# Cosine attention and a highway layer on one core: v loaded as fp32 by the hardware queues, squares and gate steps spread over engines, early products of zeros, another order

## The chip, the core and the metric

The kernel runs on one core of a Trainium2 chip. The core has five instruction queues: TensorE (PE, the matrix products; its weight loads are shown as PEld), VectorE (DVE), ScalarE (ACT), GpSimd (POOL) and SyncE (SP). SP, ACT and POOL also issue DMA transfers, which 16 DMA engines carry out. The metric is the device time of one execution in microseconds. Three timed runs of the kernel before gave 280.35, 280.48 and 280.91 us.

## The reference

Eight batches, twelve heads, 448 positions, 64 numbers per head; then a layer on 3584 rows of 768. All inputs and the result are fp32.

```python
q_n = q / (np.linalg.norm(q, axis=-1, keepdims=True) + 1e-06)
k_n = k / (np.linalg.norm(k, axis=-1, keepdims=True) + 1e-06)
scores = np.matmul(q_n, k_n.transpose(0, 1, 3, 2)) / tau        # tau = 0.1
scores = scores - np.max(scores, axis=-1, keepdims=True)
attn = np.exp(scores)
attn = attn / (np.sum(attn, axis=-1, keepdims=True) + 1e-09)
attn_out = np.matmul(attn, v)                                   # (8, 12, 448, 64)
x = attn_out.transpose(0, 2, 1, 3).reshape(8 * 448, 768)
H = np.maximum(x @ w_h, 0.0)
T = 1.0 / (1.0 + np.exp(-(x @ w_t + b_t)))
out = T * H + (1.0 - T) * x
```

## The kernel before

Work goes batch by batch (b = 0 to 7). Within a batch the twelve heads form three groups (g = 0 to 2) of four. Operands of the products are fp16, sums fp32.

For each group and for q and k: **sq** squares the tile (L359 on ACT, L362 on POOL for four of k's tiles, L364 on DVE for one half), **rd** sums the squares of a head (L370, DVE), **y** is the inverse root of these sums, by logarithm and exponent on ACT for batch 0 (L396 and L399), and by Newton steps on DVE otherwise (L381 to L388). **qn** and **kn** (L413, mostly POOL) multiply by y and make fp16. A turn brings 64-number rows onto partitions: by products with the identity (L425) and a copy from the banks (L433, DVE), or, for q from batch 3 and k from batch 5, by a transposing DMA on SP's queue (L428, tiles qT and kT).

The scores are products on TensorE (L468 and L478; L549 in batch 0), ACT takes their exponent (L471, L481, L564), TensorE multiplies with v (L499, L507, L577), where a column of ones beside v gives the sum, and DVE divides (L514, L516, L583) into x. The factor 1/tau is within the norm of q: its squares are scaled by tau before the sum.

**v** is loaded by three transfers per batch on POOL's queue (L315 to L317, into `vr`, fp16: the transfer converts). DVE (L439, **vc**) and POOL (L449, **vt**) copy it into `vp`, the layout that the product reads, with the ones and zeros around it. Both `vr` and `vp` have two buffers.

The layer has four pieces per batch, of 128 rows (the fourth half as much). x is turned by a transposing DMA on SP's queue (L628, `xT`; batch 0 by TensorE). L659 and L662 multiply with wt and wh. **za** adds the bias (L699, DVE), **th** is the hyperbolic tangent on ACT (L713), **gt** makes the gate 0.5 th + 0.5 (L715, DVE), **hm** is relu minus x (L710, DVE), **gg** multiplies (L735, DVE), **out** adds x (L737, POOL), and SP stores (L744, L747). `z` and `tt` have two buffers, `hm` three, `os` four. The last two pieces take another way (L703 to L706, L721).

All q loads stand on SP's queue, k on POOL's (batch 0: SP and ACT), w on POOL's. At the beginning TensorE runs 18 products of a tile of zeros, `wz` (L280), which DVE clears first (L264).

Nothing is scheduled at build time: each step is an operation with a number in the order in which the code makes them, `ORDER` lists these numbers in the order in which they are written into the queues, and `SLOTS` gives the buffer that each new tile takes. An engine takes its own in that order. `HOLD` puts single loads behind a named operation, and `PORT` names the kinds on DVE and POOL between which a POOL step is put behind the last DVE step ahead of it in the order.

```python
            for o in pl.ordered(ORDER, SLOTS):
                n = len(nc.cur_bb.bb.instructions)
                o.fn()
```

Of the kernel before, what the change touches and what calls it, by code (L numbers as in the profile page):

```python
# [78 lines left out]
SLOTS = {  # L79
    "qr": "01010101",  # L80
    "kr": "0120121",
    "kn": "012012021012021012102210",
    "vr": "01010101",
    "vp": "01010101",
    "sq": "012012020121021201201210120210121020120201021020",
# [94 lines left out]
def kernel(  # L180
# [110 lines left out]
    def v_src(b):  # L291
        return v[b].rearrange("h (l j) d -> l h j d", j=NJ)
# [554 lines left out]
```

## Time and profile before

| | |
|---|---|
| timed runs, median (lowest to highest) | 280.48 us (280.35 to 280.91) |
| the profiled execution: its own time / its span | 279.05 us / 277.2 us |
| mean granted TensorE clock | 0.946 |
| busy: PE, DVE, ACT, POOL | 238.2, 213.9, 204.7, 169.5 us |
| bytes read from and written to HBM | 39.12 MB, 11.01 MB |
| DMA queues: hardware (q1) / software (q0, POOL's) | 33.57 MB, 53.5% / 13.08 MB, 35.1% of 16 engines' span |

Times in the profile count from the start of the span. A group's row gives the line, the engine, the operation, the tiles out and in, their shapes and how many there were; then their busy time and the mean of one in ns; then the engine's idle time just before them and what ended it. In a row of the timeline the idle time before the instruction stands in brackets with what released it. Lines are those of the kernel before; in the kernel after the change the same code stands three lines higher or so. L12 is line 12.

### The profile page before, as it was taken

To read this page: it belongs to the slowest core of one execution; us is meant where nothing else is said; L and a number is where in the kernel's file an instruction comes from. 1 tells how busy PE (TensorE), PEld (TensorE's weight loads), DVE (VectorE), ACT (ScalarE), POOL (GpSimd) and SP (SyncE) were. 2 spreads that over 40 slices of the span, in tenths; PEclk is the share of its full clock that TensorE was granted. 3 is DMA by queue.
4 is the path that set the end of the run, shared out by engine and by line. 5 is a ranking of instruction groups with operands and counts; after the bars stand their busy time and mean duration, and the time that the engine had idled before them with its cause. 6 is when DMAs were issued, how large, how long until landed. Compare 5 with 4: busy or idle time off the path is not lost.

```text
span 277.2 us, 8206 instructions
## 1 busy us (share of the span) xinstructions
PE 238.2 (86%) x3447; PEld 146.5 (53%) x3447; DVE 213.9 (77%) x367; ACT 204.7 (74%) x253; POOL 169.5 (61%) x161
## 2 busy tenths in 40 slices
PE   8256799699989899498896999997999989999990
PEld 3135676365755565255554466564645755575640
DVE  3889669779999988639997678789776766446894
ACT  3396898799998989658788599996889568870230
POOL 2495829939837899138879645789348941330550
PEclk9856599999999999979999899999999999999998
DMA  7999599998599769996889979999879467238565
GB/s 229 290 176 254 161 246 204 216 275 104 60 162 263 115 177 223 135 197 120 125 228 166 201 136 175 194 272 196 113 177 163 82 147 162 66 75 194 139 154 144
DMA packets 77398, 47.93 MB, mean 173 GB/s; under 512 B 53040, under 2 KB 74160, under 8 KB 77360
## 3 DMA queue, kind: packets, MB, share of 16 engines
q1 hardware_dynamic: 54128, 33.57, 53.5%
q0 software_dynamic: 22800, 13.08, 35.1%
q10 hardware_dynamic: 432, 0.75, 0.8%
q8 instruction: 27, 0.44, 0.7%
q14 instruction: 11, 0.09, 0.1%
HBM read 39.12 MB, written 11.01 MB: 181 GB/s over the span
## 4 chain that ended last, share of the span: by engine, by line
PE 43%; DMA 21%; DVE 15%; POOL 10%; issue 6%; ACT 2%; DVEq 0%; POOLq 0%; ACTq 0%
PE banks L662 22%; DMA xT<-x 9%; PE banks L468 6%; PE banks L499 6%; DMA kr<-in_k_dram 6%; PE banks L659 4%; DMA qT<-qn 4%; POOL qn L413 3%; POOL kn L413 3%; DVE tt L715 2%; DVE hm L735 2%; DMA qr<-in_q_dram 2%; ACT E L471 2%; DVE x L516 2%; PE banks L478 1%
## 5 line engine op out<-in xcount | busy, mean ns | idle before, releaser
L471 ACT ACTIVATE E<-banks 128x896 f16<-128x896 f32 x126 | 109.7, 917 | 22.0 <-PE banks L468 20.0
L662 PEld LDWEIGHTS <-xT 128*128 128x128 f16 x576 | 51.9, 99 | 49.9 <-issue 14.1
L737 POOL TENSOR_TENSOR os<-x,hm 128x768 f32<-128x768 f16 (+1 forms) x30 | 44.7, 1493 | 42.9 <-DVE hm L735 20.2
L662 PE MATMUL banks<-wt,xT 128*128 128x384 f16 x288 | 55.3, 333 | 7.0 <-DMA xT<-x 6.9
L662 PE MATMUL banks<-wh,xT 128*128 128x384 f16 x288 | 55.6, 332 | 0.9 <-DVE hm L710 0.9
L370 DVE TENSOR_REDUCE n<-sq 128x14 f32<-128x896 f32 (+1 forms) x50 | 51.1, 1037 | 6.3 <-ACT sq L359 6.3
L413 POOL TENSOR_TENSOR qn<-qr,y 128x896 f16<-128x896 f32 (+1 forms) x24 | 41.0, 1710 | 23.2 <-issue 10.8
L413 POOL TENSOR_TENSOR kn<-kr,y 128x384 f16<-128x384 f16 (+1 forms) x42 | 40.0, 964 | 21.5 <-DVE y L388 7.8
L468 PE MATMUL banks<-qT,kT 64*64 64x448 f16 x504 | 40.0, 365 | 2.8 <-DVE x L516 1.7
L713 ACT ACTIVATE tt<-z 128x768 f16<-128x768 f32 (+1 forms) x32 | 24.2, 764 | 19.8 <-DVE z L699 19.2
L499 PE MATMUL banks<-vp,E 128*128 128x65 f16 x756 | 37.7, 194 | 0.0
L499 PEld LDWEIGHTS <-E 128*128 128x128 f16 x756 | 34.0, 97 | 6.5 <-issue 3.6
L710 DVE SCALAR_TENSOR_TENSOR hm<-banks,x 128x768 f16<-128x768 f32 (+1 forms) x30 | 25.7, 858 | 13.1 <-PE banks L662 10.2
L499 PE MATMUL banks<-vp,Et 128*128 128x65 f16 x252 | 34.3, 192 | 0.0
L699 DVE TENSOR_TENSOR z<-banks,bias 128x768 f32<-128x768 f32 x24 | 22.9, 952 | 9.6 <-PE banks L662 9.4
L359 ACT ACTIVATE sq<-qr 128x896 f32<-128x896 f32 (+1 forms) x24 | 22.1, 935 | 5.3 <-DMA qr<-in_q_dram 3.7
L499 PEld LDWEIGHTS <-Et 128*128 128x128 f16 x252 | 24.9, 99 | 0.0
L715 DVE TENSOR_SCALAR tt<-tt 128x768 f16<-128x768 f16 (+1 forms) x32 | 21.8, 683 | 2.7 <-ACT tt L713 2.7
L516 DVE TENSOR_TENSOR x<-banks,rd 128x896 f16<-128x896 f32 x21 | 22.9, 1089 | 0.5
L481 ACT ACTIVATE Et<-banks 128x896 f16<-128x896 f32 x21 | 19.0, 917 | 4.5 <-PE banks L478 4.4
L468 PEld LDWEIGHTS <-kT 64*64 64x64 f16 x504 | 12.6, 105 | 17.7 <-issue 15.2
L359 ACT ACTIVATE sq<-kr 128x896 f32<-128x896 f16 x17 | 16.1, 951 | 5.1 <-DMA kr<-in_k_dram 4.7
(74 smaller groups left out, 301.4 us busy)
## 6 DMA issues: line engine op xcount, KB each, us to landing
out_dram<-os SPq DMA_DIRECT2D x47, 192.0 KB, 3.3
qr<-in_q_dram SPq DMA_DIRECT2D x6, 1344.0 KB, 7.4
kr<-in_k_dram POOLq DMA_DIRECT2D x7, 672.0 KB, 12.9
vr<-in_v_dram POOLq DMA_DIRECT2D x8, 384.0 KB, 7.7
qr<-in_q_dram SPq DMA_DIRECT2D x6, 448.0 KB, 6.8
vr<-in_v_dram POOLq DMA_DIRECT2D x8, 288.0 KB, 9.4
out_dram<-os SPq DMA_DIRECT2D x15, 96.0 KB, 2.6
wt<-in_moe_w_t_dram POOLq DMA_DIRECT2D x1, 1152.0 KB, 13.8
```

The lines of the kernel that those rows point to most:

```text
L359: nc.scalar.activation(dst, src, AF.Square, scale=sc)
L370: nc.vector.reduce_sum(R("n2", b)[:, c : c + 7 * n], a, axis=AX.X)
L413: ENG[eng].tensor_mul(o[:, :, t0:t1, :], a, y.unsqueeze(3).to_broadcast([128, hi - lo, t1 - t0, D]))
L468: nc.tensor.matmul(R("B", ("S", n, c))[64 * x : 64 * x + 64, t, 0:S], lhsT=keys(i, s, t, 2 * c + x), rhs=queries(t, s), start=True, stop=True)
L471: op("ACT", f"exp {n} {c}", lambda c=c, n=n: nc.scalar.activation(R("E", n)[:, 14 * c : 14 * c + 14, :].rearrange("l (t j) x -> l t (j x)" ...
L499: nc.tensor.matmul(U[:, 2 * c + t, :], lhsT=(E if m < NC else Et)[:, at : at + 2, :].rearrange("l j x -> l (j x)"), rhs=vp[:, 3 * t + m if ...
L516: op("DVE", f"ev14 {i}", lambda: nc.vector.tensor_mul(R("x", b)[:, :, 128 * g : 128 * g + 128].rearrange("l j (s d) -> l s j d", s=2), U_( ...
L662: nc.tensor.matmul(R("B", at)[:, mh, 0:MH], lhsT=xT[:, cc, :], rhs=w_[:, cc, MH * mh : MH * mh + MH], start=(cc == 0), stop=(cc == CC - 1))
L710: step("hm", n, lambda n=n, P=P: nc.vector.scalar_tensor_tensor(out=cut(R("hm", g), n), in0=P(n), scalar=0.0, in1=xs(n), op0=ALU.max, op1= ...
L713: op("ACT", f"th{nb} {g}", lambda: nc.scalar.activation(R("tt", g)[:, 0:W], R("z", g)[:, 0:W], AF.Tanh, scale=0.5), r=[("z", g), ("t0",)], ...
L715: op("DVE", f"gt{nb} {g}", lambda: nc.vector.tensor_scalar(out=R("tt", g)[:, 0:W], in0=R("tt", g)[:, 0:W], scalar1=0.5, scalar2=0.5, op0=A ...
L737: op("POOL", f"out{nb} {g}", lambda: nc.gpsimd.tensor_add(view(R("os", g)), xs(None), view(R("hm", g))), r=[("gg", g), xk], w=[("os", g)], ...
```

## The change

1. `vr` becomes fp32, and its three loads per batch leave POOL's queue: 22 of 24 go to SP's, two to ACT's. The copies into `vp` convert to fp16, five of DVE's vc now run on POOL, and one of POOL's vt on DVE.
2. A table, `MOVED`, sets another engine for 46 operations. Of 48 tiles of squares (beside the split ones of group 0 of batch 0) 12 are on POOL and 7 on DVE, where POOL had four and DVE none; ten of 24 wide gate steps and four of eight narrow ones go from DVE to POOL; three loads of q go from SP's queue to ACT's.
3. The squares are no longer scaled by tau; the exponent of the scores multiplies by 1/tau instead. On DVE a square is now a plain product of two operands.
4. After the 18 products of zeros stand 23 more, and two times six later among the first products.
5. `ORDER`, `SLOTS` and `HOLD` are new throughout, and gg is no longer among `PORT`. The operands of the final addition are swapped.

```diff
--- before
+++ after
-1 4 24 25 2 6 26 0 242 21 17 27 14 19 29 3 16 18 12 28 9 22 13 5 8 11 40 15 20 42 7 10 43 36 38 41 37 39 52 53 44 68
...
+3 24 25 242 26 0 27 2 29 28 4 30 9 31 7 6 32 13 15 240 11 5 16 12 21 19 22 40 42 18 14 8 41 20 38 10 1498 1499 1500
+1501 1502 1503 1504 1505 1506 1507 1508 1509 1510 1511 1512 1513 1514 1515 1516 1517 1518 1519 1520 36 39 43 37 44 52
...
 SLOTS = {
...
-HOLD = {239: 44, 240: 57, 241: 252, 429: 121, 610: 56, 788: 57, 966: 53, 1141: 537, 1316: 161}
-PORT = ("nt", "gt", "gg", "vc", "qn", "kn", "vt", "out", "cx", "ou")
+HOLD = {240: 0, 429: 107, 610: 53, 966: 795, 1141: 89, 1316: 843}
+MOVED = {'sq1 q 0 0 1': 'ACT', 'sq1 k 0 0 1': 'DVE', 'sq2 q 0 1 0': 'POOL', 'gt6 0': 'POOL', 'gt6 1': 'POOL', 'gt6 2': 'POOL', 'gt3 3': 'POOL', 'ldq 1 0': 'ACT', 'ldq 1 2': 'ACT', 'sq2 q 1 1 0': 'POOL', 'sq2 q 1 2 0': 'POOL', 'vc6 1 0 1': 'POOL', 'gt6 4': 'POOL', 'gt3 7': 'POOL', 'sq2 q 2 0 0': 'DVE', 'sq2 k 2 2 0': 'POOL', 'gt6 9': 'POOL', 'sq2 q 3 1 0': 'DVE', 'sq2 k 3 1 0': 'POOL', 'sq2 k 3 2 0': 'POOL', 'vc6 3 0 1': 'POOL', 'ldq 4 0': 'ACT', 'sq2 k 4 1 0': 'DVE', 'sq2 k 4 2 0': 'POOL', 'gt6 16': 'POOL', 'gt6 18': 'POOL', 'ldv4 5': 'ACT', 'sq2 k 5 0 0': 'POOL', 'sq2 k 5 2 0': 'POOL', 'vc6 5 0 1': 'POOL', 'gt6 20': 'POOL', 'gt6 21': 'POOL', 'gt3 23': 'POOL', 'sq2 q 6 1 0': 'DVE', 'sq2 q 6 2 0': 'POOL', 'sq2 k 6 2 0': 'DVE', 'vc6 6 0 0': 'POOL', 'vt 6 0': 'DVE', 'ldv4 7': 'ACT', 'sq2 k 7 0 0': 'DVE', 'sq2 q 7 1 0': 'DVE', 'sq2 k 7 1 0': 'POOL', 'sq2 k 7 2 0': 'POOL', 'vc6 7 0 1': 'POOL', 'gt6 30': 'POOL', 'gt3 31': 'POOL'}
+PORT = ("nt", "gt", "vc", "qn", "kn", "vt", "out", "cx", "ou")
...
     def op(self, eng, name, fn, w=(), r=(), u=(), mode=None):
-        o = Op(eng, name, fn, w, r, u, mode)
+        o = Op(MOVED.get(name, eng), name, fn, w, r, u, mode)
         o.seq = len(self.ops)
...
-    WARM, FILL, NLATE = 18, (), 2
+    WARM, FILL, NLATE = 18, (23, 6, 6), 2
...
-        qr=(2, [128, 6, 448], FP32), kr=(3, [128, 6, 448], FP16), kn=(3, [128, NJ, 2, D], FP16), vr=(2, [128, NH, 256], FP16),
+        qr=(2, [128, 6, 448], FP32), kr=(3, [128, 6, 448], FP16), kn=(3, [128, NJ, 2, D], FP16), vr=(2, [128, NH, 256], FP32),
...
+    on = []
...
-                ENG[eng].dma_start(d[:, :, :], a)
+                on[-1].dma_start(d[:, :, :], a)
             else:
-                ENG[eng].dma_start(d[:, gs[0] :: 3, :], a[:, :, gs[0] :: 3, :])
+                on[-1].dma_start(d[:, gs[0] :: 3, :], a[:, :, gs[0] :: 3, :])
         op(eng, f"ld{nm} {b} {gs[0]}", fn, w=[(nm + "r", b, g) for g in gs])
...
-            (4, lambda: nc.gpsimd.dma_start(vr()[0:64].rearrange("l h (c d) -> l h c d", c=4), v_src(b)[:, :, 0:4, :])),
-            (3, lambda: nc.gpsimd.dma_start(vr()[64:128, :, 0:192].rearrange("l h (c d) -> l h c d", c=3), v_src(b)[:, :, 4:7, :])),
-            (1, lambda: nc.gpsimd.dma_start(vr()[64:128, 1::2, 192:256], v_src(b)[:, 1::2, 3, :]))):
-            op("POOL", f"ldv{n} {b}", fn, w=[("vr", b, n)])
+            (4, lambda: on[-1].dma_start(vr()[0:64].rearrange("l h (c d) -> l h c d", c=4), v_src(b)[:, :, 0:4, :])),
+            (3, lambda: on[-1].dma_start(vr()[64:128, :, 0:192].rearrange("l h (c d) -> l h c d", c=3), v_src(b)[:, :, 4:7, :])),
+            (1, lambda: on[-1].dma_start(vr()[64:128, 1::2, 192:256], v_src(b)[:, 1::2, 3, :]))):
+            op("SP", f"ldv{n} {b}", fn, w=[("vr", b, n)])
...
-    SQV = ()
-    SQP = tuple(("k", b, 1) for b in range(2, 6))
...
         i = (nm, b, g)
-        sc = tau if nm == "q" else 1.0
-        engs = SPLIT.get(i, (("DVE" if i in SQV else "POOL" if i in SQP else "ACT"),))
+        engs = SPLIT.get(i, ("ACT",))
         n = 3 - len(engs)
         for t, eng in enumerate(engs):
             ts = slice(t, t + n)
 
-            def fn(eng=eng, ts=ts):
+            def fn(ts=ts):
                 src = source(nm, b, g)[:, ts]
                 dst = R("sq", i).rearrange("l (t x) -> l t x", t=2)[:, ts]
-                if eng == "ACT":
-                    nc.scalar.activation(dst, src, AF.Square, scale=sc)
-                elif eng == "POOL":
-                    assert sc == 1.0
-                    nc.gpsimd.tensor_mul(dst, src, src)
+                if on[-1] is nc.scalar:
+                    nc.scalar.activation(dst, src, AF.Square)
                 else:
-                    nc.vector.scalar_tensor_tensor(out=dst, in0=src, scalar=sc * sc, in1=src, op0=ALU.mult, op1=ALU.mult)
+                    on[-1].tensor_mul(dst, src, src)
             op(eng, f"sq{n} {nm} {b} {g} {t}", fn, r=[token(nm, b, g), ("t6",)], w=[("sq", i, t)])
...
-                nc.vector.tensor_copy(
+                on[-1].tensor_copy(
                     R("vp", b)[:, p0:p1, 3 * t : 3 * t + 3, 0:D],
                     R("vr", b)[:, 6 * t + p0 : 6 * t + p1, 0:192].rearrange("l p (c d) -> l p c d", c=NC))
...
-                    R("E", n)[:, 14 * c : 14 * c + 14, :].rearrange("l (t j) x -> l t (j x)", t=2), R("B", ("S", n, c))[:, :, 0:S], AF.Exp),
+                    R("E", n)[:, 14 * c : 14 * c + 14, :].rearrange("l (t j) x -> l t (j x)", t=2), R("B", ("S", n, c))[:, :, 0:S], AF.Exp, scale=1.0 / tau),
...
-                op("DVE", f"gt{nb} {g}", lambda: nc.vector.tensor_scalar(
+                op("DVE", f"gt{nb} {g}", lambda: on[-1].tensor_scalar(
                     out=R("tt", g)[:, 0:W], in0=R("tt", g)[:, 0:W], scalar1=0.5, scalar2=0.5, op0=ALU.mult, op1=ALU.add),
...
-        op("POOL", f"out{nb} {g}", lambda: nc.gpsimd.tensor_add(view(R("os", g)), xs(None), view(R("hm", g))),
+        op("POOL", f"out{nb} {g}", lambda: on[-1].tensor_add(view(R("os", g)), view(R("hm", g)), xs(None)),
            r=[("gg", g), xk], w=[("os", g)], u=[("hm", g)])
...
+    for i, n in enumerate(FILL):
+        for j in range(n):
+            op("PE", f"wf {i} {j}", constant(("F", i)), r=[("wz",)], w=[("B", ("F", i))], mode="F")
...
             for o in pl.ordered(ORDER, SLOTS):
                 n = len(nc.cur_bb.bb.instructions)
+                on.append(ENG[o.eng])
                 o.fn()
```

More of the change, by code (lines that the diff above doesn't have):

```diff
@@ L93 @@
-    "Et": "012012021021021021021",
+    "qn": "012012012012012012012012",
+    "qT": "01230123012301203123012",
+    "kT": "01230123012301230213021",
+    "E": "012012121020102000210210210210120120210210121021012012012",
+    "Et": "012012012012010210210",
     "rd": "010101010101010101010101010101010",
     "x": "012012012",
-    "xT": "01234021342013420143241302143201",
-    "z": "01011010011010101010101000101010",
-    "tt": "01010100100110101010010010110101",
-    "hm": "01202012201201201201201202102012",
@@ L283 @@
         op("PE", f"wm {i}", constant(("W",)), r=[("wz",)], w=[("B", ("W",)), ("wm",)], mode="F")
-    for i, n in enumerate(FILL):
-        for j in range(n):
-            op("PE", f"wf {i} {j}", constant(("F", i)), r=[("wz",)], w=[("B", ("F", i))], mode="F")
     def q_src(t, b):
@@ L481, in scores @@
         op("ACT", f"expt {i}", lambda: nc.scalar.activation(
-            R("Et", i).rearrange("l (t j) x -> l t (j x)", t=2), R("B", ("St", i))[:, :, 0:S], AF.Exp),
+            R("Et", i).rearrange("l (t j) x -> l t (j x)", t=2), R("B", ("St", i))[:, :, 0:S], AF.Exp, scale=1.0 / tau),
            r=[("B", ("St", i))], w=[("Et", i)])
@@ L564, in fe @@
                 nc.scalar.activation(R("E", e).rearrange("l j x -> l (j x)")[:, o : o + 2 * m].rearrange("l (t x) -> l t x", t=2),
-                                     R("B", A)[:, :, 0:m], AF.Exp)
+                                     R("B", A)[:, :, 0:m], AF.Exp, scale=1.0 / tau)
             op("ACT", f"ex{wide(ss[0]) // 64} {n}", fe, r=[("B", A)], w=[("E", e, s) for s in ss] + [("E", e, 0)])
```

28 lines of the change are left out of this document (14 added, 14 removed), and 108 rows, old and new, of the table ORDER.

## Prediction

> **What bounds the kernel now.** I read the page first, then busy time in stretches of 4 us, then the chain of waits and the timeline at the places where TensorE stands still, and last the groups that the change moves.
>
> ```profile
> span 277.2 us, 8206 instructions
> PE 238.2 (86%) x3447; PEld 146.5 (53%) x3447; DVE 213.9 (77%) x367; ACT 204.7 (74%) x253; POOL 169.5 (61%) x161
> PE 43%; DMA 21%; DVE 15%; POOL 10%; issue 6%; ACT 2%; DVEq 0%; POOLq 0%; ACTq 0%
> ```
>
> TensorE is the fullest engine, yet the chain that ended last lies on it for only 43% and on DMA for 21%. So I look for the 39 us (277.2 less 238.2) in which it is idle. Columns of the next view: stretch, its length, busy time (instructions) of PE, PEld, DVE, ACT, POOL, then granted clock, DMA share, GB/s.
>
> ```profile
> 8.00:12.00 4.00, 0.00 (x0) 0.00 (x0) 3.36 (x7) 2.19 (x4) 1.10 (x1) 0.96 1.16 280
> 12.00:16.00 4.00, 2.49 (x39) 1.97 (x42) 2.97 (x5) 1.62 (x3) 4.00 (x7) 0.50 1.02 239
> 16.00:20.00 4.00, 2.00 (x48) 1.49 (x39) 3.55 (x4) 3.97 (x9) 3.53 (x4) 0.50 1.37 166
> 20.00:24.00 4.00, 2.89 (x44) 2.20 (x45) 3.77 (x7) 4.00 (x7) 3.80 (x4) 0.50 1.17 216
> 48.00:52.00 4.00, 2.86 (x40) 1.61 (x39) 1.94 (x5) 1.68 (x3) 3.94 (x4) 1.00 1.47 196
> 112.00:116.00 4.00, 1.82 (x44) 1.09 (x43) 3.76 (x10) 3.57 (x5) 0.00 (x0) 1.00 1.40 163
> 116.00:120.00 4.00, 2.14 (x11) 1.13 (x12) 0.00 (x0) 0.00 (x0) 0.00 (x0) 0.69 1.37 200
> 148.00:152.00 4.00, 1.92 (x49) 1.32 (x43) 3.04 (x4) 3.92 (x5) 3.64 (x4) 0.95 1.28 141
> 188.00:192.00 4.00, 2.05 (x31) 1.11 (x33) 4.00 (x4) 1.68 (x3) 3.80 (x4) 1.00 1.24 206
> 240.00:244.00 4.00, 4.00 (x51) 2.07 (x49) 2.41 (x5) 3.69 (x5) 0.00 (x0) 1.00 0.00 0
> ```
>
> Three kinds of loss: a start (8 to 24 us) with TensorE half idle and its clock at 0.50; a hole at 48 to 52; holes at 112, 148 and 188 where the DMA share is above 1.2. From 240 on TensorE is full at full clock, so what is gained earlier reaches the end.
>
> **The start.** The second head group's norms, not POOL, set the pace, and ACT's queue delays them:
>
> ```profile
> 12.19 0.93 PE L425 MATMUL banks<-ident,qn 128*128 128x128 f16 x7 [5.12 <-POOL qn L413]
> 10.12 0.23 ACT L399 ACTIVATE y<-tu 128x28 f32<-128x28 f32 x1
> 12.25 0.57 DVE L413 TENSOR_TENSOR kn<-E,y 128x192 f16<-128x192 f32 x1
> 14.41 0.95 ACT L359 ACTIVATE sq<-kr 128x896 f32<-128x896 f16 x1 [2.38 <-DMA kr<-in_k_dram]
> 16.44 0.23 ACT L399 ACTIVATE y<-tu 128x28 f32<-128x28 f32 x1
> 16.75 1.70 POOL L413 TENSOR_TENSOR qn<-qr,y 128x896 f16<-128x896 f32 x1 [0.47 <-ACT y L399]
> ```
>
> ACT waits 2.38 us for k of batch 1 while the squares and the logarithm of group 1 stand behind that wait; POOL's scaling of group 1 starts only when y is there (16.67). ACT's rows, before:
>
> ```order
> L399 ACTIVATE y_78<-tu_81 128x28
> L359 ACTIVATE sq_75<-qr_61 128x896
> L359 ACTIVATE sq_73<-E_95 128x896
> L359 ACTIVATE sq_74<-kr_63 128x896
> L359 ACTIVATE sq_75<-E_96 128x896
> L396 ACTIVATE tu_82<-n_76,eps 128x28
> L399 ACTIVATE y_78<-tu_82 128x28
> ```
>
> and of the change, from the same y on:
>
> ```order
> L396 ACTIVATE y_78<-tu_81 128x28
> L359 ACTIVATE sq_73<-E_95 128x896
> L305 DMA qr_62<-in_q_dram 128x2x448
> L359 ACTIVATE sq_74<-E_96 128x896
> L393 ACTIVATE tu_82<-n_76,eps 128x28
> L396 ACTIVATE y_78<-tu_82 128x28
> L305 DMA qr_62<-in_q_dram 128x2x448
> L359 ACTIVATE sq_75<-qr_61 128x896
> L359 ACTIVATE sq_73<-kr_63 128x896
> ```
>
> The square of q group 1 went to POOL, and the one of batch 1's k stands behind group 1's y. Without that wait y of group 1 is set by Vector's work after y of group 0. That one came at 10.35; now a square of half a tile, about 0.6, moves from Vector's queue behind the first sum to ACT, so 9.8. Then come two scalings like the one at 12.25 (1.2 together), two sums of squares at 1.07 (row below), and logarithm and exponent at about 0.55: 13.7, or 3.0 us earlier. Against it stand the early products:
>
> ```profile
> 1.26 5.81 PE L280 MATMUL banks<-wz 128*128 128x512 f16 x18 [1.26 <-DVE wz L264]
> 2.62 1.15 DVE L264 MEMSET vp<- 128x36 f16 x4 [0.17 <-issue]
> 4.97 1.61 PEld L280 LDWEIGHTS <-wz 128*128 128x128 f16 x8 [0.17 <-issue]
> ```
>
> The zero tile is now cleared behind eight memsets of vp (two such groups, 2.3 us), so products start near 3.6 instead of 1.26. Of the 53, 40 stand ahead of the first transposes. Before, ten of 18 took the first 3.71 us (4.97 less 1.26) and eight the next 1.61, 0.20 each. So ten slow ones to 7.3 and 30 fast ones to 13.3: the first transposes start 1.1 us later than 12.19, and 13 more products (2.6 us) stand between the next ones. In return those run at full clock: the 7.4 us of work in the three rows at 0.50 shrink by up to half, 3.7. I count these two as even.
>
> The Trainium skill, "TensorE: Matmul & The Clock Gate", Part 1, says the activity window is free-running at some 3.4 us. By it the full clock may come one to two windows after 3.6, an estimate of 7.0 to 10.4, and the 40 products would end at 13.4 to 15.2; the trace's 3.71 lies within, and no run here shows the spread.
>
> **The hole at 48.** Pieces of the chain (start, us, what), and the instruction that waited:
>
> ```profile
> 34.07 16.36 DMA kr<-in_k_dram
> 50.51 1.79 ACT L359 ACTIVATE sq<-kr 128x896 f32<-128x896 f16 x2 [2.32 <-DMA kr<-in_k_dram]
> 108.16 9.66 DMA xT<-x
> 143.12 8.46 DMA xT<-x
> 191.65 6.86 DMA qT<-qn
> ```
>
> The k load of batch 2 is issued at 34.07 and lands 16.36 us later, behind wh and among v. POOL's rows before:
>
> ```order
> L413 TENSOR_TENSOR kn_66<-kr_63,y_79 128x4x128
> L317 DMA vr_70<-in_v_dram 64x6x64
> L321 DMA wh<-in_moe_w_h_dram 128x6x768
> L300 DMA kr_64<-in_k_dram 128x6x448
> L316 DMA vr_70<-in_v_dram 64x12x192
> L315 DMA vr_70<-in_v_dram 64x12x256
> ```
>
> and of the change:
>
> ```order
> L410 TENSOR_TENSOR qn_85<-qr_61,y_78 128x896
> L324 DMA wh<-in_moe_w_h_dram 128x6x768
> L361 TENSOR_TENSOR sq_75<-qr_62 128x896
> L361 TENSOR_TENSOR sq_74<-qr_62 128x896
> L303 DMA kr_64<-in_k_dram 128x6x448
> L303 DMA kr_65<-in_k_dram 128x6x448
> L410 TENSOR_TENSOR kn_66<-kr_63,y_79 128x3x128
> ```
>
> The load (kr_64) now stands ahead of batch 1's scaling, behind two squares (3.4 us), and no v is in that queue: about 27 (13.7, and 13.3 us of scalings, squares, casts and two weight issues on POOL ahead of it, an estimate from their rows). Even at 16.36 us it lands at 43, so ACT's 2.32 us of waiting goes. ACT also loses two squares of this stretch (1.8). First term: 3.0 at the start, of which ACT's full row (16 to 24) passes on perhaps half, 1.5; plus 2.3; plus little of the squares, since DVE is nearly as full: **-4**, bounds -7 and 0.
>
> **The holes at 112, 148, 188.** There the transposes on SP's queue are slow: 9.66, 8.46 and 6.86 us, where the median is 3.6. What ran beside the first:
>
> ```profile
> 108.01 0.89 POOL L300 DMA_DIRECT2D kr<-in_k_dram  x1
> 108.89 0.77 POOL L316 DMA_DIRECT2D vr<-in_v_dram  x1
> xT<-x SPq DMA_TRANSPOSE x28, 3.6
> vr<-in_v_dram POOLq DMA_DIRECT2D x8, 384.0 KB, 7.7
> ```
>
> k and v go out in one burst. The change separates v from k, but puts it ahead of transposes. SP before, from batch 4's q on:
>
> ```order
> L300 DMA qr_61<-in_q_dram 128x6x448
> L428 DMA_TRANSPOSE qT_86<-qn_84 128x7x128
> L628 DMA_TRANSPOSE xT_106<-x_104 128x3x128
> L744 DMA out_dram<-os_119 64x384 x2
> L300 DMA qr_62<-in_q_dram 128x6x448
> L428 DMA_TRANSPOSE qT_87<-qn_83 128x7x128
> ```
>
> and now at the same transposes:
>
> ```order
> L743 DMA out_dram<-os_118 64x768 x2
> L319 DMA vr_69<-in_v_dram 64x12x192
> L425 DMA_TRANSPOSE qT_86<-qn_83 128x7x128
> L320 DMA vr_69<-in_v_dram 64x6x64
> L319 DMA vr_70<-in_v_dram 64x12x192
> L740 DMA out_dram<-os_120 64x384 x2
> L303 DMA qr_62<-in_q_dram 128x6x448
> ```
>
> Five times a large piece of v stands right ahead of a transpose. The bytes read are the same; those written into the tile double. TensorE's idle time in the rows at 112, 116, 148 and 188 is 8.0 us. I take a third of it back: **-3**, bounds -8 (all) and +10 (five transposes each late by 7.7 less 3.6, half of it on the path).
>
> **Work moved between engines.**
>
> ```profile
> L370 DVE TENSOR_REDUCE n<-sq 128x14 f32<-128x896 f32 x46 | 48.9, 1074 | 3.1 <-ACT sq L359 3.1
> L737 POOL TENSOR_TENSOR os<-x,hm 128x768 f32<-128x768 f16 x23 | 38.3, 1671 | 35.1 <-DMA out_dram<-os 15.8 <-DVE hm L735 13.2 <-DVE tt L715 6.0
> L715 DVE TENSOR_SCALAR tt<-tt 128x768 f16<-128x768 f16 x24 | 18.1, 759 | 2.1 <-ACT tt L713 2.1
> L439 DVE COPY vp<-vr 128x1152 f16<-128x1152 f16 x14 | 9.2, 657 | 0.0
> L449 POOL COPY vp<-vr 64x384 f16<-64x384 f16 x16 | 8.3, 520 | 7.9 <-DVE hm L735 4.6 <-issue 1.3 <-DMA vr<-in_v_dram 0.7
> L362 POOL TENSOR_TENSOR sq<-kr 128x896 f32<-128x896 f16 x4 | 6.7, 1676 | 3.9 <-DVE n L370 3.8
> L316 POOL DMA_DIRECT2D vr<-in_v_dram x8 | 6.2, 771 | 0.0
> L315 POOL DMA_DIRECT2D vr<-in_v_dram x8 | 6.2, 772 | 0.0
> L439 DVE COPY vp<-vr x18: 338/453/1899, 24.0 to 233.0; 128x1152 f16<-128x1152 f16 x14, 128x576 f16<-128x576 f16 x4
> ```
>
> POOL loses 24 issues of v, a third kind beside the two rows being like them, some 18 us, and gains eight squares (13.4), ten wide and four narrow gate steps and five casts. No row has its one-input price at 768: twice the 0.52 for 384 gives 1.04 below, the two-input 1.67 above; I take 1.04, the nearest kind. That is 12.5, and the casts (three times 0.52) 7.8: POOL goes from 169.5 to 185, to 198 at the top. ACT loses 15 squares (14) and issues five loads. DVE loses ten gate steps at 0.76, four narrow ones and five copies at 0.66, gains seven squares at about 1.07, and its nine wide casts cost 0.66 if they run like the copy, 1.38 if like the sum of squares (1.074 over 896, for 1152): between -5 and +3. None becomes the fullest. What may show is the gate: a step on POOL can wait behind a scaling, so I add **+1.5**, bounds 0 and +9. The scale of 1/tau in the exponent and the swapped operands of the final sum add no instruction.
>
> The Trainium skill, "SBUF — State Buffer", Who interferes with whom, says POOL and two-port Vector copies or casts lock each other out for a whole instruction. The 1,899 ns copy beside a median of 453 agrees. More POOL work is then a loss at DVE too; by it the +1.5 would be nearer its upper bound.
>
> **Sum.** -4 -3 +1.5 = -5.5 on the profiled execution: 279.05 (span 277.2 and 1.85 around it) becomes 273.55. The three timed runs have their median 1.43 above that execution, so 280.48 becomes **275.0**.
>
> **Rivals.**
> - All three losses go (start -6, holes -6.5, gate +0.5): 268.5. For it: TensorE has 39 us to give. Against: every byte still has to move. 0.15.
> - The early products are in the way: the first transposes wait until 15 and the start gains nothing; -3 +1.5 gives 279. For it: 40 products in a row. 0.12.
> - The gain is handed back, other transposes being late instead: 280.5. 0.06.
> - Slower: v ahead of transposes in SP's ring. Start -4, holes 0, five late transposes cost 4.1 each, and with a third on the path +7, gate +1.5: 285. It decides against the change once more than 0.5 us of each 4.1 reaches TensorE. 0.12.
> - Slower: gates on POOL at 1.67, each behind one scaling (1.7): 14 times 2.6 us late, of which a quarter, +9, reaches TensorE through two-deep rings: 282.5. 0.12.
> - The forecast, 272 to 278: 0.43.
>
> Within 0.2% is what a measurement here cannot tell from no change. Faster 0.43 + 0.15 + 0.12 = 0.70, same 0.06, slower 0.24. The range cuts the outer half of the best case and most of the worst: 268.5 to 283.5; the forecast's own is 272 to 278.
>
> **What would show it.** Right: group 1's y near 13.7; no hole at 48; a clock near 1.0 from 12 to 24; fewer transposes over 8 us; POOL near 185. Wrong: first transposes after 15; ACT idle behind late exponents; transposes waiting directly behind v; POOL's gate step above 1.5 us or DVE waiting for it.

## The result

| | before | predicted | after |
|---|---|---|---|
| time, median of five runs | 280.48 us (280.19 to 280.91) | 275.0 us (268.5 to 283.5; the forecast's own 272 to 278) | 277.04 us (276.24 to 278.47) |
| ratio to before | | 0.980 | 0.988, 95% interval 0.985 to 0.991 |
| the profiled execution | 279.05 us | 273.55 us | 278.47 us, the longest of its five |

The change makes the kernel faster, by 3.4 us where 5.5 were forecast. On a second chip its ratio was 0.992 (0.987 to 0.996, the last experiment), so the gain is 0.8 to 1.2%. One execution of a later kernel took 332.78 us at a granted clock of 0.656, and the ratios leave out such executions and all that lie over 1.5% above the shortest of their kernel on that chip.

The two profiled executions are only 0.58 us apart: the one of before is shorter than all its five timed runs, the one of the change is the longest of its five. Their traces show what moved, but not where the 3.4 us of the medians come from. The page of the profile after:

```profile
span 276.7 us, 8304 instructions
PE 241.6 (87%) x3482; PEld 148.9 (54%) x3482; DVE 223.9 (81%) x356; ACT 194.5 (70%) x238; POOL 182.3 (66%) x163
PE 42%; DVE 28%; DMA 10%; POOL 9%; issue 6%; SPq 3%; ACT 1%; DVEq 0%; POOLq 0%; ACTq 0%
```

The third row is the chain that ended last. DMA's share of it fell from 21% to 10%, Vector's rose from 15% to 28% (12% and 32% in a second profile of the change, the last experiment). The stretches of 4 us that the prediction showed of before, in the kernel after (same columns, core's busy time of PE, PEld, DVE, ACT, POOL, then clock, DMA share, GB/s):

```profile
16.00:20.00 4.00, 3.45 (x50) 2.23 (x48) 3.06 (x5) 3.03 (x6) 2.30 (x4) 1.00 1.12 238
20.00:24.00 4.00, 2.09 (x81) 1.59 (x80) 4.00 (x7) 4.00 (x6) 2.27 (x3) 1.00 1.13 242
24.00:28.00 4.00, 1.98 (x39) 1.82 (x39) 4.00 (x6) 1.54 (x2) 3.87 (x4) 0.61 1.15 230
28.00:32.00 4.00, 3.54 (x78) 3.08 (x76) 4.00 (x11) 2.56 (x4) 2.57 (x3) 0.50 1.16 212
48.00:52.00 4.00, 3.89 (x73) 2.80 (x72) 4.00 (x7) 3.39 (x5) 4.00 (x4) 1.00 1.16 236
112.00:116.00 4.00, 4.00 (x39) 2.04 (x37) 4.00 (x8) 3.55 (x5) 2.95 (x4) 1.00 1.24 176
148.00:152.00 4.00, 4.00 (x34) 1.79 (x33) 4.00 (x8) 2.52 (x4) 3.85 (x4) 1.00 1.04 213
188.00:192.00 4.00, 4.00 (x46) 2.24 (x43) 3.92 (x5) 3.06 (x4) 3.71 (x5) 1.00 0.79 163
```

The holes at 48, 112, 148 and 188 are gone. The start is not: the clock is full until 24, but TensorE is half idle from 20 to 28, and the clock is at 0.61 from 24 and at 0.50 from 28, which it had before from 12 to 24. The stretch became shorter as well as later: the clocks of the seven rows from 12 to 40 us add up to a loss worth 20 us at half clock before and 14 us after. And the rest has changed sides more than once. First the kernel before, then the kernel after, in three longer stretches:

```profile
56.00:112.00 56.00, 53.39 (x848) 33.19 (x850) 51.84 (x86) 52.49 (x65) 43.34 (x40) 1.00 0.92 171
112.00:160.00 48.00, 38.94 (x508) 22.34 (x507) 35.96 (x56) 33.72 (x42) 31.29 (x26) 0.93 1.00 168
200.00:240.00 40.00, 39.00 (x545) 23.04 (x542) 27.06 (x46) 30.39 (x38) 23.29 (x22) 1.00 0.72 138
```

```profile
56.00:112.00 56.00, 49.19 (x781) 31.64 (x780) 53.16 (x77) 46.47 (x57) 43.91 (x38) 1.00 1.03 219
112.00:160.00 48.00, 42.60 (x603) 24.78 (x604) 44.66 (x67) 38.19 (x46) 39.62 (x33) 1.00 1.13 191
200.00:240.00 40.00, 37.19 (x510) 21.89 (x507) 20.05 (x32) 28.33 (x37) 22.48 (x21) 0.96 0.81 140
```

TensorE lost 4.2 us from 56 to 112, gained 3.7 from 112 to 160 and lost 1.8 from 200 to 240. The holes at the transposes were filled, and many small waits came ahead of them. By the view of waits TensorE stood 10.1 us behind DMA before and 7.5 after, but 9.8 behind Vector before and 12.5 after (sums of the rows by releaser). Of the latter, 1.3 and 3.9 us are the first product's wait for the tile of zeros; without it the sums are 8.5 and 8.6. What grew is Vector's part from 56 to 112, from 1.8 to 4.0 us.

The longest DMA pieces in the chain, which were 16.36, 9.66 and 8.46 us, are now these:

```profile
152.05 6.78 DMA xT<-x
187.07 7.05 DMA vr<-in_v_dram
204.88 8.08 DMA out_dram<-os
216.42 5.55 DMA kT<-kn
```

The third of them is a store, and it hands part of the gain back. POOL's final sum waits until the store lands and its tile is free, the scaling of k stands behind that sum on POOL, and k's transpose, the fourth piece, behind the scaling. Of the 3429 products that both kernels share, 2896 had started by 220 us in the change and 2832 before; by 230 us it was 2967 and 2969, and up to the end the two profiled executions stay level. The same store is long in other kernels with the new order too (7.84 us in the second profile of the change).

### The profile page after: what moved, and what is told of

Its sections match the earlier page's. It is cut to its first block, busy times and chain, and to the rows that moved or that the text cites. A ratio compares the mean times of both kernels' runs of the same rounds, so it can differ in the third digit from the quotient of the medians.

```text
span 276.7 us, 8304 instructions
## 1 busy us (share of the span) xinstructions
PE 241.6 (87%) x3482; PEld 148.9 (54%) x3482; DVE 223.9 (81%) x356; ACT 194.5 (70%) x238; POOL 182.3 (66%) x163
## 4 chain that ended last, share of the span: by engine, by line
PE 42%; DVE 28%; DMA 10%; POOL 9%; issue 6%; SPq 3%; ACT 1%; DVEq 0%; POOLq 0%; ACTq 0%
PE banks L659 16%; DVE n L367 6%; PE banks L496 5%; PE banks L465 5%; PE banks L656 4%; PE banks L285 4%; POOL kn L410 3%; POOL qn L410 3%; DMA out_dram<-os 3%; DMA vr<-in_v_dram 3%; DVE vp L436 3%; DMA xT<-x 2%; DVE hm L731 2%; DVE hm L707 2%; DMA kT<-kn 2%
## 5 line engine op out<-in xcount | busy, mean ns | idle before, releaser
L659 PEld LDWEIGHTS <-xT 128*128 128x128 f16 x576 | 51.1, 97 | 45.8 <-issue 12.1
L733 POOL TENSOR_TENSOR os<-hm,x 128x768 f32<-128x768 f16 (+1 forms) x30 | 44.6, 1493 | 30.4 <-DVE hm L731 16.9
L659 PE MATMUL banks<-wt,xT 128*128 128x384 f16 x288 | 54.0, 327 | 3.5 <-DMA xT<-x 3.2
L410 POOL TENSOR_TENSOR kn<-kr,y 128x384 f16<-128x384 f16 (+1 forms) x42 | 40.6, 983 | 17.5 <-DVE y L385 6.9
L496 PE MATMUL banks<-vp,E 128*128 128x65 f16 x756 | 38.4, 194 | 0.0
L465 PEld LDWEIGHTS <-kT 64*64 64x64 f16 x504 | 13.4, 104 | 26.5 <-issue 21.0
L561 ACT ACTIVATE E<-banks 128x1024 f16<-128x1024 f32 (+2 forms) x21 | 18.5, 917 | 6.7 <-PE banks L574 3.7
L731 DVE TENSOR_TENSOR hm<-tt,hm 128x768 f16<-128x768 f16 (+1 forms) x30 | 20.7, 693 | 1.4 <-POOL tt L712 1.2
L285 PE MATMUL banks<-wz 128*128 128x512 f16 x53 | 13.8, 422 | 3.9 <-DVE eps L269 3.9
## 6 DMA issues: line engine op xcount, KB each, us to landing
kr<-in_k_dram POOLq DMA_DIRECT2D x7, 672.0 KB, 10.3
vr<-in_v_dram SPq DMA_DIRECT2D x8, 576.0 KB, 10.3
```

The lines of the kernel that those rows point to most:

```text
L285: return lambda: nc.tensor.matmul(R("B", at)[:, 0, :], lhsT=wz[:, 0:128], rhs=wz[:, 128:640], start=True, stop=True)
L410: on[-1].tensor_mul(o[:, :, t0:t1, :], a, y.unsqueeze(3).to_broadcast([128, hi - lo, t1 - t0, D]))
L465: nc.tensor.matmul(R("B", ("S", n, c))[64 * x : 64 * x + 64, t, 0:S], lhsT=keys(i, s, t, 2 * c + x), rhs=queries(t, s), start=True, stop=True)
L496: nc.tensor.matmul(U[:, 2 * c + t, :], lhsT=(E if m < NC else Et)[:, at : at + 2, :].rearrange("l j x -> l (j x)"), rhs=vp[:, 3 * t + m if ...
L659: nc.tensor.matmul(R("B", at)[:, mh, 0:MH], lhsT=xT[:, cc, :], rhs=w_[:, cc, MH * mh : MH * mh + MH], start=(cc == 0), stop=(cc == CC - 1))
L731: op("DVE", f"gg{nb} {g}", lambda: nc.vector.tensor_mul(R("hm", g)[:, 0:W], R("tt", g)[:, 0:W], R("hm", g)[:, 0:W]), r=[("gt", g), ("hm", ...
```

## The experiments

On the experiments' chips the executions of one kernel lie up to 2% from their median (274.15 to 286.29 us around 280.16 in one). So the ratios to the kernel before on the same chip decide, and where few executions stand behind one the single times are given.

### The extra products: left out, and started earlier

```diff
-    WARM, FILL, NLATE = 18, (23, 6, 6), 2
+    WARM, FILL, NLATE = 18, (), 2
```

(and the numbers 1498 to 1532 out of `ORDER`, with their banks in `SLOTS`.)

> The changed kernel without its 35 extra products of zeros; the 18 early ones stay. Theory (the extra products hold TensorE until 14.6 us, later than y of group 1 allows): the first transposes start near 12.5 us in place of 14.45, the clock is 0.50 from 12 to about 20, and the time falls by 1 to 2 us, to 275.0 to 276.0. Rival (the two effects cancel, as the prediction counted them): 276.6 to 277.5. Second rival (the extra products pay through the clock): 278 to 280.

The second kernel clears the zero tile, operation 4, first on Vector:

```diff
-3 24 25 242 26 0 27 2 29 28 4 30 9 31 7 6 32 13 15 240 11 5 16 12 21 19 22 40 42 18 14 8 41 20 38 10 1498 1499 1500
+4 3 24 25 242 26 0 27 2 29 28 30 9 31 7 6 32 13 15 240 11 5 16 12 21 19 22 40 42 18 14 8 41 20 38 10 1498 1499 1500
```

> The changed kernel with one memset moved: the zero tile of the products is cleared ahead of the vp memsets on Vector, as before the change. The products then start near 1.3 in place of 3.9 us and end near 12 to 12.5. Theory (the late end of the products costs): first transposes near 12.5 to 13.5, time 275.5 to 276.3. Rival (group 2's late q load, not group 1, sets the first 28 us): y of group 2 stays at 19.9 and the time at 276.7 to 277.5.

Measured: 277.32 us, ratio 0.985 (0.978 to 0.992), and 279.11 us, ratio 0.988 (0.979 to 0.998). Neither differs from the whole change by what can be told, so the rivals hold by the ratio. By the single time 279.11 us is above both ranges of the second experiment, and its rival's condition was not met either: y of the third group came at 18.6, not 19.9. TensorE's timeline in the change, without the products, and with the zeros first:

```profile
3.91 10.70 PE L285 MATMUL banks<-wz 128*128 128x512 f16 x40 [3.91 <-DVE eps L269]
14.45 0.55 PE L422 MATMUL banks<-ident,qn 128*128 128x128 f16 x7
26.42 0.93 PE L422 MATMUL banks<-ident,qn 128*128 128x128 f16 x7 [2.02 <-POOL qn L410]
```

```profile
11.46 0.55 PE L419 MATMUL banks<-ident,qn 128*128 128x128 f16 x7 [1.03 <-POOL ident masks.py:199]
26.54 0.93 PE L419 MATMUL banks<-ident,qn 128*128 128x128 f16 x7 [3.05 <-POOL qn L407]
```

```profile
11.78 0.55 PE L422 MATMUL banks<-ident,qn 128*128 128x128 f16 x7
26.24 0.93 PE L422 MATMUL banks<-ident,qn 128*128 128x128 f16 x7 [2.90 <-POOL qn L410]
```

The first transposes move by 3 us, from 14.45 to 11.46 or 11.78, and those of the third q group start at 26.2 to 26.5 in all three. Before the change that group was turned at 23.86. What makes it late stands on POOL, in the kernel after (two rows), without the products, and with the zeros first:

```profile
24.03 0.54 POOL L446 CAST vp<-vr 64x384 f16<-64x384 f32 x1 [1.76 <-DMA vr<-in_v_dram]
24.65 1.71 POOL L410 TENSOR_TENSOR qn<-qr,y 128x896 f16<-128x896 f32 x1
```

```profile
24.12 0.57 POOL L443 CAST vp<-vr 64x384 f16<-64x384 f32 x1 [3.01 <-DMA vr<-in_v_dram]
```

```profile
23.81 0.50 POOL L446 CAST vp<-vr 64x384 f16<-64x384 f32 x1 [2.83 <-DMA vr<-in_v_dram]
```

In the change the third group's y is there at 19.9 (before 20.2), and POOL waits 1.76 us for v ahead of the scaling of q, which began at 22.09 before. Where y comes sooner, POOL only waits longer for v. v's three transfers of this batch, which landed by 20.67 before, land at about 23.9 in all three. With v back in POOL's queue (below) the third group is turned at 25.16, so v is a cause of its lateness. It does not set the whole time: that kernel is 2.5 us ahead of the change at 40 us and level with it at 44.

### Vector relieved: squares to ScalarE, gates back to Vector, all engines as before

Three kernels change entries of `MOVED`. In the first the seven squares of DVE go back to ACT (`...` leaves entries out):

```diff
-MOVED = {... 'sq2 q 2 0 0': 'DVE', ... 'sq2 q 3 1 0': 'DVE', ... 'sq2 k 7 0 0': 'DVE', 'sq2 q 7 1 0': 'DVE', ...}
+MOVED = {...}
```

> The changed kernel with its seven squares of Vector back on ScalarE (order as it is). Theory (Vector at 53 of 56 us from 56 to 112 has become the full engine): DVE's busy time falls by 9 to 10 us to about 214, ACT's grows by 6.5 to 201, and the time falls by 2 to 4 us to 273 to 275. Rival (ScalarE, at 93% in the same stretch, takes the place, or the waits for scores grow): 277 to 279.

In the second the gate steps and wide casts of POOL go back to DVE:

```diff
-MOVED = {... 'gt6 0': 'POOL', 'gt6 1': 'POOL', 'gt6 2': 'POOL', 'gt3 3': 'POOL', ... 'vc6 7 0 1': 'POOL', ...}
+MOVED = {...}
```

> The changed kernel with its 14 gate steps and five casts of v that went to POOL back on Vector. POOL falls from 182 to about 166. Theory (Vector is the full engine from 56 to 160): DVE's busy time grows by 8 to 13 us and the time by 3 to 5 us, to 280 to 282. Rival (POOL's two-input work beside Vector costs Vector as much as it takes off it): Vector's other steps shorten, DVE grows by under 5 us, and the time is 276 to 278.

In the third every moved operation goes back to its engine before:

```diff
-MOVED = {'sq1 q 0 0 1': 'ACT', ... 'gt3 31': 'POOL'}
+MOVED = {'sq2 k 2 1 0': 'POOL', 'sq2 k 3 1 0': 'POOL', 'sq2 k 4 1 0': 'POOL', 'sq2 k 5 1 0': 'POOL'}
```

> The changed kernel with the engines of before: squares on ScalarE but for four on POOL, gate steps, wide casts of v on Vector, q loads on SP; v stays in fp32 on SP's queue, and the order and the extra products stay. Theory (the moves cost, +1.5 in the prediction, nearer its bound of +9 by Vector's grown time): ratio to before 0.975 to 0.985. Rival (ScalarE was the engine that had to be relieved): ScalarE at 205 and the ratio 0.992 to 1.002.

Measured: squares to ACT 279.19 us, ratio 0.989 (0.980 to 0.998); gates to DVE 279.83 us beside 281.69 of before, 276.67 to 281.95 and no interval; engines as before 277.91 us, ratio 0.991 (0.988 to 0.994). None is told from the change; by the ratio the first is where its rival put it, and the third lies between its two ranges, next to the rival's. The theory that Vector had become the bound is not borne out. Squares to ACT took Vector from 223.9 to 217.0 us busy, and TensorE did no more from 56 to 112 than in the change (48.45 us of 56 beside 49.19, in an execution of 282.99 us, the longest of its four), but Vector itself went only from 53.16 to 51.13 us in that stretch. More telling is the kernel before: Vector was as full there, 51.84 us, with TensorE at 53.39. Gates to DVE brought Vector to 229.2 us, 5.3 more, between what theory and rival had, and POOL down to 166.1 as expected; its two shortest executions took 276.67 and 278.76 us. With all engines as before TensorE had 49.04 us from 56 to 112, the busy times being

```profile
PE 241.4 (87%) x3482; PEld 148.9 (54%) x3482; DVE 215.6 (78%) x367; ACT 204.8 (74%) x253; POOL 152.1 (55%) x137
```

So moving 46 operations took 10.3 us off ScalarE, put 30.2 on POOL and 8.3 on Vector, and left the time where it was. Vector got more although about as much was taken off it as was added: by the rows with the engines as before, ten wide and four narrow gate steps and five casts, some 11 us, for squares and a cast of some 10. In the change, and with the engines as before:

```profile
L712 DVE TENSOR_SCALAR tt<-tt 128x768 f16<-128x768 f16 x14 | 9.5, 677 | 1.8 <-ACT tt L710 1.8
L378 DVE TENSOR_SCALAR y<-n 128x84 int32<-128x84 int32 x6 | 3.6, 601 | 0.0
```

```profile
L712 DVE TENSOR_SCALAR tt<-tt 128x768 f16<-128x768 f16 x24 | 11.8, 492 | 2.2 <-ACT tt L710 2.1
L378 DVE TENSOR_SCALAR y<-n 128x84 int32<-128x84 int32 x6 | 1.2, 195 | 0.0
```

The means hide two kinds of step. Of the six small steps of 84 columns in the change four take 192 to 198 ns, and two take 1144 and 1683. These two start while a step of POOL runs and end 0.06 us after it, as the later one shows:

```profile
157.14 1.68 POOL L361 TENSOR_TENSOR sq<-kr 128x896 f32<-128x896 f16 x1 [0.35 <-POOL qn L410]
157.20 1.68 DVE L378 TENSOR_SCALAR y<-n 128x84 int32<-128x84 int32 x1
```

With the engines as before none of the six meets a step of POOL, and all take 187 to 204 ns. The wide gate step, too, takes 342 to 360 ns where it meets none and up to 1887 in the change where it meets one. So what counts is what a step meets, which the order sets, not how much POOL has to do in all: the kernel before, with 169.5 us on POOL, has 439 for the small step, and the same changed kernel profiled again has 703, and 861 for the gate step. The 2.3 us that the row of gate steps gave back for ten steps fewer lie within that spread (9.5 and 12.1 us for the same fourteen).

### The path of v: POOL's queue in the new order, SP's in the old

```diff
-        vr=(2, [128, NH, 256], FP32),
+        vr=(2, [128, NH, 256], FP16),
...
+MOVED = {... 'ldv4 0': 'POOL', 'ldv3 0': 'POOL', 'ldv1 0': 'POOL', ... 'ldv1 7': 'POOL'}
```

> The changed kernel with v as before: loaded as fp16 through POOL's queue (24 issues), its copies on chip fp16 to fp16; order, engines and extra products of the change. Theory (taking v off POOL's queue is what made the holes smaller, the prediction's -3): POOL at about 198 busy, DVE about 216, the holes return and the ratio to before is 0.997 to 1.005. Rival (the path of v is neutral, the gain came from the order): 0.984 to 0.992, as with the whole change.

and the kernel before with this part alone:

```diff
-        vr=(2, [128, NH, 256], FP16),
+        vr=(2, [128, NH, 256], FP32),
...
-            (4, lambda: nc.gpsimd.dma_start(vr()[0:64].rearrange("l h (c d) -> l h c d", c=4), v_src(b)[:, :, 0:4, :])),
+            (4, lambda: nc.sync.dma_start(vr()[0:64].rearrange("l h (c d) -> l h c d", c=4), v_src(b)[:, :, 0:4, :])),
...
-            op("POOL", f"ldv{n} {b}", fn, w=[("vr", b, n)])
+            op("SP", f"ldv{n} {b}", fn, w=[("vr", b, n)])
```

> The kernel before with one part of the change: v in fp32 on SP's queue (24 loads), its casts on chip; order, slots and engines of before. Theory (v off POOL is worth 3 us in any order): ratio 0.986 to 0.993, POOL at about 151 busy. Rival (v in SP's queue holds up transposes, and the order was not made for it): ratio 1.005 to 1.03.

Measured: the change with v on POOL 285.88 us, ratio 1.018 (1.014 to 1.023); the kernel before with v on SP 291.77 us, ratio 1.041 (1.037 to 1.045). Both are slower than before, by more than either theory had it, where the two together are 1% faster. So v's path is worth 3% in the new order and costs 4% in the old one; neither part has a price of its own.

The loss in the old order is not what the slower rival described, transposes held up behind v. TensorE's waits for transposes add up to 9.3 us there and 10.1 before, the medians of the transposes are within 0.1 us of before, and more than half of the loss is there before SP issues its first transpose, at 85.32: the product that starts at 53.16 in the trace of before is reached 5.75 us later, and by 60 us the kernel is 7.5 us behind. What came late are loads. Rows of the kernel before with v on SP:

```profile
36.50 19.69 DMA kr<-in_k_dram
58.91 0.59 PE L549 MATMUL banks<-qT,kT 64*64 64x64 f16 x28 [4.67 <-ACT E L471]
91.91 13.97 DMA vr<-in_v_dram
PE banks L662 <- DMA xT<-x: 5.9, 2, 3.6
PE banks L577 <- DMA qr<-in_q_dram: 4.2, 1, 4.2
```

and the same product in the kernel before:

```profile
53.16 0.41 PE L549 MATMUL banks<-qT,kT 64*64 64x64 f16 x28 [2.29 <-ACT E L471]
```

k of batch 2 lands at 56.2 instead of 50.4, and ScalarE waits 6.87 us for it; v of the first batch lands at 26.05 instead of 20.67, a load of q holds TensorE for 4.2 us, and later a piece of v takes 13.97. In all TensorE stands 15.6 us behind DMA (before 10.1). In the new order with v on POOL it is not DMA:

```profile
PE banks L656 <- DVE kT L430: 3.0, 1, 3.0
PE banks L422 <- POOL kn L410: 2.5, 2, 1.9
PE banks L659 <- DMA xT<-x: 2.4, 1, 2.4
L319 POOL DMA_DIRECT2D vr<-in_v_dram x8 | 6.2, 781 | 0.0
```

The third row is its only wait for DMA; it stands 21.2 us behind Vector instead (12.5 in the change). POOL has 199.0 us of work, the 24 issues of v being three rows like the last, some 18 us, between scalings on which Vector and TensorE wait. At one place this can be followed: at 63.48 an issue of v stands ahead of the scalings of q and k on POOL, and TensorE's wait for kn at 68.97 is 1.90 us, where the change has one of 0.74 at 67.23. So it fits these rows that the new path of v buys POOL's time, but how the 3% add up was not followed further.

### Parts of the change in the kernel before: products, and the k load of batch 2

```diff
-    WARM, FILL, NLATE = 18, (), 2
+    WARM, FILL, NLATE = 18, (23, 6, 6), 2
```

(and their numbers put into `ORDER` behind the 18, behind the first transposes of q, and behind those of k, and their banks into `SLOTS`.)

> The kernel before with the 35 extra products of zeros (23 behind the first 18, six each behind the first two groups of transposes) and nothing else. The products start at 1.3 there and 41 of them should end near 11.5, ahead of the first transposes at 12.2. Theory (they raise the clock): granted clock near 1.0 from 12 to 20, ratio 0.990 to 0.996. Rival (as in the first experiment, where the time did not move: what the clock gives, the 12 products among the first transposes take, and the start waits for norms anyway): 0.998 to 1.002.

The next kernel has one number moved in the order of before, 430 (the load) ahead of 280 (the first scaling of batch 1's k). POOL's rows:

```order
 L449 COPY vp_71<-vr_69 64x2x3x64 x2
+L300 DMA kr_64<-in_k_dram 128x6x448
 L413 TENSOR_TENSOR kn_66<-kr_63,y_79 128x3x128
```

> The kernel before with one instruction moved: the load of batch 2's k is issued on POOL ahead of batch 1's scalings (near 28 us, in place of 34.07), so ahead of wh and of v. Theory (the hole at 48 is this load, the prediction's 2.3): it lands near 40 to 44, ScalarE's wait of 2.32 us at 48 goes, and the ratio to before is 0.990 to 0.995. Rival (the hole only moves: another load or transpose is late in its place): 0.997 to 1.003.

and both edits together:

> The kernel before with the 35 extra products and the early load of batch 2's k, nothing else: the two parts of the change that need neither its order nor its engines nor v on SP. Theory (the two gains are of different places and add): ratio 0.975 to 0.985, below the whole change's 0.988. Rival (each is given back at late transposes near 112 to 165 us, as in the runs of the products alone that took 280 and more): 0.990 to 1.003, with a wide spread.

Measured: with the products 0.983 (0.975 to 0.991), six executions from 274.15 to 286.29 us, median 280.16. With the early load 0.979 (0.972 to 0.985), 274.68 and 276.02 us, the other four 279.2 to 279.4. With both 0.976 (0.969 to 0.984), 273.02 to 283.10 us, median 280.16 without the one of 332.78. Each of these ratios rests on the two shortest of six executions (274.15 and 277.04, 274.68 and 276.02, 273.02 and 276.39). The medians lie only 0.3, 0.7 and 0.4% below those of before (281.06 on one chip, 281.17 on the other). So the theories hold for the shortest executions, the rivals for the others, and neither part is shown to be worth 2%. How a gain is lost shows in the execution with the early load that was profiled, one of 279.4 us. The hole at 48 is gone (TensorE 4.00 of 4 us, 2.86 before), and then:

```profile
159.77 0.61 PE banks L499 x16
161.65 6.79 DMA kT<-kn
176.00 0.61 PE banks L659 x6
```

```profile
163.21 0.60 PE banks L499 x16
175.97 0.63 PE banks L659 x6
```

The second fence is the same chain in the kernel before. At the products of x16 the early load has its kernel 3.44 us ahead, more than the 2.3 of the prediction; then a transpose of k takes 6.79 us, which the chain of before does not have, and at 176 the two are level to 0.03 us. In this trace, what comes early into the stretch waits there for a late transpose. The profiled execution with the products, one of 279.94 us, is 7.4 us ahead at about 155 and has lost that by the end too.

In the kernel before the products start at 1.3 us, and the start changes. TensorE, in stretches as above:

```profile
12.00:16.00 4.00, 4.00 (x30) 2.25 (x29) 2.92 (x6) 1.98 (x3) 3.98 (x6) 1.00 1.06 232
24.00:28.00 4.00, 2.67 (x50) 1.92 (x49) 3.49 (x11) 1.48 (x2) 1.00 (x2) 0.50 1.03 288
```

The clock is full from 12 to 20, where it was 0.50, at 0.57 from 20 and back at 0.50 from 24: here, too, a stretch at half clock follows once the products are over.

### The rule between Vector and POOL

```diff
-PORT = ("nt", "gt", "vc", "qn", "kn", "vt", "out", "cx", "ou")
+PORT = ()
...
-        self.port = eng in ("DVE", "POOL") and (kind in PORT or kind == "sq")
+        self.port = eng in ("DVE", "POOL") and kind in PORT
```

> The changed kernel without the rule that makes POOL's operation wait for the last such operation of Vector ahead of it in the order; waits for data stay. Theory (the two engines slow each other where they overlap, and the rule only keeps some of that apart): POOL's idle time falls, but Vector's busy time grows from 224 by 4 to 10 us, and the time by 1 to 4 us. Rival (the rule costs waits and saves nothing): Vector at 222 to 226 and the time 1 to 3 us lower, ratio 0.975 to 0.985.

Measured: 292.56 us, ratio 1.035 (1.029 to 1.041), 12 to 14 us above the change on the same chip (by the ratios and by the medians). The theory had the direction and a quarter of the size; the rival falls. Vector's busy time is 237.9, 14 above the change, and TensorE stands 27.7 us behind it. Its rows by shape, where the change has 752, 317 and 1075 ns:

```profile
L731 DVE TENSOR_TENSOR hm<-tt,hm 128x768 f16<-128x768 f16 x23 | 20.5, 895 | 2.3 <-POOL tt L712 2.1
L381 DVE TENSOR_TENSOR tu<-y 128x84 f32<-128x84 f32 x12 | 6.5, 539 | 0.2
L367 DVE TENSOR_REDUCE n<-sq 128x14 f32<-128x896 f32 x46 | 48.7, 1075 | 0.5 <-ACT sq L359 0.4
```

These two kinds with two operands in SBUF grow, and the squares of k do, from 1323 to 1579 ns; the squares of q, also with two, do not (1460 and 1436). The sum of squares with one operand does not move by a nanosecond. The Trainium skill, "SBUF — State Buffer", Who interferes with whom, says just this: a Vector instruction with two SBUF inputs contends with a POOL instruction that reads SBUF, one with a single input outside the two-port modes does not. The trace agrees but for the squares of q. The price of leaving the rule out is 12 to 14 us in this order, which was made with the rule; in another order it can differ.

### The change once more

No edit; the changed kernel beside the last three kernels, on the same chip.

> The changed kernel as it is, on the same chip as the three others, as the measure for them: ratio 0.984 to 0.992 to before, by its first five runs. By the theory that its order and its path of v are made for each other, its spread should be no wider than before's.

Measured: 278.22 us, median of twelve, ratio 0.992 (0.987 to 0.996). The ratio is at the edge of what was expected. The spread was expected to be no wider than before's and is a little wider: 275.88 to 282.45 beside 277.03 to 283.13. The kernels before with the early load and with both parts, on this chip, have lower single times (274.68 and 273.02) and higher medians (279.19 and 280.16), as has the one with the products on another chip (274.15 and 280.16), so none of them can be said to beat the change.

## Why the prediction was right, and where it was not

It said faster, 275.0 us and 272 to 278 for its own case; 277.04 came. The sum was 2.0 us too good, and its terms fared worse than the total: that the sum came so near is in part luck.

- **Start, 1.5.** Wrong in what sets it. y of group 1 came at 13.4 (13.19 and 0.23 of its exponent) where 13.7 was forecast, but the way there was not the one forecast: Vector's sums were done at 12.07, and the logarithm then stood behind a square on ScalarE that waited 1.56 us for k. And the third group was not looked at: its scaling on POOL slipped from 22.09 to 24.65, 1.76 us of it behind a wait for v, which now comes over SP. The clock was full from 12 to 24 as forecast; the stretch at half clock came behind that, shorter, instead of going away.
- **Early products, counted even.** Right by the ratios, 0.985 to 0.988 without them or with them sooner, and for a reason that was not given: the third group is turned at the same time with and without them. They ended at 14.61, not 13.3. The count of ten slow products was right, 9 or 10 at 427 ns from start to start and 30 at 216; what was off is the start, 3.91 for 3.6, and the prices, 0.37 and 0.20, which came from rows of weight loads. The other kernels' 8 to 13 slow products show the spread. By the Trainium skill's free-running window ("TensorE: Matmul & The Clock Gate", Part 1) the estimate was 13.4 to 15.2, which holds the 14.61.
- **Hole at 48, 2.3.** The hole went, as said. The load was not issued at 27 but at 31.96, late by the same third group on POOL, and it was early enough still. Alone in the kernel before it is worth 3.4 us by 160 and 0 by 176 in one trace. The step that failed is that a gain of one place reaches the end because TensorE is full from 240 on: between the two lie transposes that take it back, and in the change's own trace the store at 204.88 does.
- **Holes at 112, 148 and 188, 3.** The size came out near, 2.6 us less behind DMA (10.1 to 7.5), but that is luck: the third was a guess, the idle time in these rows, 8.0 us, went wholly, and the 2.6 count all of TensorE's waits for DMA. Nor was the cause right. With v back in POOL's queue, k and v in one burst, TensorE's wait for DMA is 2.4 us; so what became shorter behind DMA came with the order, as far as it shows beside a later POOL. And the transposes did not get faster: eight take over 8 us in the change and three before, and their medians rose from 3.6 to 4.4 (x), 4.2 to 5.4 (q) and 3.2 to 3.9 us (k). Eight stand directly behind a piece of v, the prediction's own sign of being wrong, yet TensorE waited less for them.
- **Moved work, +1.5.** POOL was right (182.3 for 185; gate step 0.84 for 1.04 and cast 1.26 for 1.56 us). Vector was mis-sized: -5 to +3 became +10. Squares took 1.40 us for 1.07 (9.8 us for seven), the wide casts 0.99, and steps that met one of POOL's were held. That warning of the prediction came true for Vector's busy time. In time it is within what can be told, 0.991 with the old engines beside 0.988 and 0.992: +1.5 was neither confirmed nor refuted.

The rivals: "products in the way" fell with the first two experiments. "v ahead of transposes" had the cost but not the path: v on SP costs 4% in the order of before, by loads that land late. In the new order the transposes take 0.7 to 1.2 us longer in the median, not 4.1, and the order as a whole gains. "The gain is handed back" happened in part, in the profiled execution at 200 to 240, though there it was a store ahead of a transpose. "Gates on POOL at 1.67" fell: 0.84. The case of all losses going fell with the start.

Not settled: why TensorE has only 47.7 to 49.2 us of work from 56 to 112 in every kernel with the new order, whichever engines do the squares and gates, and 48.1 also in the old order with v on SP, where before had 53.4. The order itself, the single loads held back by `HOLD`, gg taken out of `PORT`, the scale in the exponent and the swapped operands had no run of their own. So it is shown that the gain hangs on v's path in the new order, and that a gain remains without the extra products (0.985) and without the moved operations (0.991). Why v's path pays in this order is argued only.

## What to carry to other kernels

Parts of a change that comes with its own order can't be priced one by one from the trace before: here v's new path is 4% slower alone, the rest 1.8% slower alone, and both together 1% faster. At a start look for the last group that must be ready, not the first, and for what else stands in its queue. A gain ahead of a stretch where transfers end late counts only as far as those come earlier too. And before a pair of traces is read for the cause of a small gain, see whether the two executions differ by as much as the medians do.

## What the runs showed of the hardware

A short Vector step that starts while a step of POOL runs can last until that ends: the same step of 84 columns took 195 ns where it met none and 1144 and 1683 ns where it met one. A rule of order between the two engines was worth 12 to 14 us of 278 in the order made with it, more than the whole change; neither was expected at that size. And TensorE's clock, at 1.00 up to 24 us behind the early products, was at 0.61 and then 0.50 behind a stretch of work at half load (20 to 28 us), so filling the first wait alone made the slow stretch shorter and later rather than removing it.
